# A spectral block on one core: its pipeline goes by one sequence instead of by two

## The chip, the cores and the metric

The kernel runs on one core of a Trainium2 chip. Its time is the device time of that core in microseconds (us), from the first to the last instruction of the program. Lower is better.

## The reference

Eight sequences of 3136 rows with 256 columns, all in float32:

```
X  = rfft(x, axis=1)                          # over the 3136 rows
Yr = Xr @ w_r - Xi @ w_i + b_r ;  Yi = Xr @ w_i + Xi @ w_r + b_i
Yr, Yi = soft_threshold(Yr, 0.01), soft_threshold(Yi, 0.01)
y  = irfft(Yr + i Yi, axis=1)
u  = y + real(fft(fft(y, axis=1), axis=2))    # over the rows and over the columns
un = (u - mean(u)) / sqrt(var(u) + 1e-6)      # along the columns
out = u + relu(un @ w_ch1) @ w_ch2            # w_ch1 256 x 1024, w_ch2 1024 x 256, float64
```

The transform of the rows of `y` is the thresholded spectrum itself, so the second transform over the rows needs no work of its own: the spectrum, transformed over the columns, is added to `y`.

## The kernel before

A transform of 3136 = 64 * 49 points goes in two stages, with n = 49 n1 + n2. The frequencies are held in 32 units; a unit has one k1 and its mirror, with 50 slots. Work passes through DRAM scratch between stages, because each stage wants another axis on the 128 partitions. The steps, each a generator in the program:

- `p1` (the first pair: `p1_first`): the sum over n1. The 128 partitions of a tile hold the 64 n1 of **two sequences**; a chunk is two values of n2 (128x512). One matmul against a table, the result (`ev`) is stored to `ad` (for the first eight units of the first pair to `a0`).
- `p2_f2`: the sum over n2, by units: `af` is loaded from `ad` (98 rows: n2 and real/imaginary), matmuls of 98x100 give the spectrum `X` and the sum of its parts `Xs`.
- `p2_w`: the complex product in three real ones (`g_w`), bias and soft threshold, giving `Y`.
- `p2_mix`: the transform of `Y` over the columns (`g_mix`, `mq`), stored to `md`.
- `p2_yt`, `p2_g2`: `Y` transposed (`g_yt`), the inverse sum over k2 (`g_g`, one matmul of 512 columns: a unit of two sequences), copied to `bev` and stored to `bd`.
- `p3_norm`: the inverse sum over n1: loads `bf` from `bd` and `mt` from `md`, a matmul, `ut` = the result + `mt`, then the norm. `p3_tr` transposes the normed `mt` (`g_ut`, giving `uth` and `utl`); `p3_mlp1` and `p3_mlp2` are the MLP in groups of up to four n2 (512 tokens): matmuls into `h`, ReLU to `hh` and `hl`, matmuls into `o`, the sum into `ut`, the store.

The frequencies go in eight steps of four units of two sequences. A step's product gives 128x400 tiles.

Precision: a float32 operand is split into a higher and a lower float32r part (`sc.copy` to the higher, a subtraction on VectorE by `lo_v` or GpSimd by `lo_g` to the lower), and `mm3` multiplies in three passes. Some work of the first pair, which runs while no MLP does, takes float32 as it is (first stage, `g_mix`, `g_g`), in one instruction pair without the splits. The MLP's float64 weights come as integer words; `split_double` makes them into two parts, in 16 blocks with eight VectorE instructions each.

What sets the order: each generator yields times of an emission clock (`T` = 10000 for a pair), and a heap merges them; so an engine's queue holds the steps of several pairs interleaved. While pair p is in its MLP (clock p + 2 to p + 3), pair p + 1 goes through `p2` and pair p + 2 through `p1`. Each engine runs its queue in order. All DMAs are issued by SyncE (SP), in order too; `behind(key)` queues a load behind a named earlier one. Buffers are few: `mt` 2, `bf` 2, `bh`/`bl` 2, `mq` 1, `X` 1, `ut` 6, and four PSUM tiles `g` for everything but the MLP.

The host permutes the rows back at the end. Nothing of that is in the time.

Of the kernel before, what the change touches and what calls it, by code (L numbers as in the profile page):

```python
# [10 lines left out]
F32 = mybir.dt.float32  # L11
# [7 lines left out]
N = 3136          # sequence length, 64 * 49; n = 49 * n1 + n2, k = k1 + 64 * k2  # L19
# [4 lines left out]
U = 32            # units of frequencies: unit u holds k1 = u and its mirror 64 - u (u = 0: k1 = 0 and 32)  # L24
# [8 lines left out]
# Constants by shape.  # L33
# [4 lines left out]
def slot_freqs(u):  # L38
    """(full index t of each slot, sign of the imaginary part against the canonical half)"""
    if u == 0:  # L40
        t = np.concatenate([64 * np.arange(25), 32 + 64 * np.arange(25)])
        return t, np.ones(50)
    t = np.concatenate([u + 64 * np.arange(25), N - (64 - u) - 64 * np.arange(24)])
    return t, np.concatenate([np.ones(25), -np.ones(24)])


def rows_n1():
    """n1 of the rows (half, n1) of the last stage: the second half runs backwards"""
    a = np.arange(32)
    return np.stack([a, 63 - a])  # L50


def tables():
    n1 = np.arange(N1)
    n2 = np.arange(N2)
    fwd = np.zeros((2, N1, 2, U, 2))      # s n1 | c u s
    inv = np.zeros((2, U, 2, 2, 2, 32))   # c u s | h s n1
    n1h = rows_n1()
    for s in range(2):
        for u in range(U):  # L60
            ph = 2 * np.pi * ((n1 * u) % N1) / N1
            if u == 0:
                alt = np.where(n1 % 2, -1.0, 1.0)
                fwd[s, :, 0, 0, s] = 1.0
                fwd[s, :, 1, 0, s] = alt
                inv[0, 0, s, :, s] = 1.0
                inv[1, 0, s, :, s] = np.where(n1h % 2, -1.0, 1.0)
            else:
                fwd[s, :, 0, u, s] = np.cos(ph)
                fwd[s, :, 1, u, s] = -np.sin(ph)  # L70
                phh = 2 * np.pi * ((n1h * u) % N1) / N1
                inv[0, u, s, :, s] = 2 * np.cos(phh)
                inv[1, u, s, :, s] = -2 * np.sin(phh)
# [27 lines left out]
    cs = np.stack([np.cos(ph), np.sin(ph)], 1)      # p | which, e  # L101
    cs[0, 1, 0] = 1.0       # the row of d = 128
# [3 lines left out]
    first = np.concatenate([fwd[:, :, :, :8].reshape(128, 32), fwd[:, :, :, 8:].reshape(128, 96)], 1)  # L106
# [9 lines left out]
# The emission's schedule, and which engine takes which part.  # L116
PAR = dict(f2w0=1.0, w00=1.069, ww0=0.988, f2w=0.395, w0=0.569, ww=0.36, end0=0.847, end=0.853, p1a=1.155, p1w=0.854, late=0.2, mlag=0.874, nrm=-1.239, tr=-0.993, yt=0.022, yts=0.185, g2=0.35, mx=0.372, mxs=0.394, cva=1.2, cvw=0.62, p1b=-0.428, p1bw=0.58, xl0=2, al0=0, y0=4, cve=1, bev=2, bf=2, mbuf=1, xsb=1, al1=0, y1=2, mxe=0, mmc=3, elg=0, f1fp=1, ev0=0, ev1=1, xe0=0, ye0=0, bev0=0, xs0=0, wc=1.291, cf=0.686, xm=3, xsm=0, mqb=1, bevb=2, evb=2, xfb=2, afb=4, eob=2, ksb=2, utb=6, tihb=1, ehb=1, hb=2, w0f=0, m0f=1, g0f=1, xm0=2, xsm0=0, xalt=1, fa=3, fs=0.6, p1c=-0.09, p1cw=0.87, trx=0, mql=0, bk=3)
# [3 lines left out]
def spectral_block(ctx: ExitStack, tc: tile.TileContext, x, w_ri, b_ri, w1, w2,  # L121
# [3 lines left out]
    NP = NB // 2  # L125
# [5 lines left out]
    dr = ctx.enter_context(tc.tile_pool(name="dr", bufs=2, space=DRAM))  # L131
# [10 lines left out]
    def copy(which, i=0):  # L142
        """0: ScalarE, 1: in turns, 2: VectorE"""
        return va.tensor_copy if which == 2 or which == 1 and i % 2 else sc.copy

# [4 lines left out]

    Q = PAR
    T = 10000       # the clock of the emission: a pair's step
    UTB = Q["utb"]
    AFB = Q["afb"]
    MLAG = PAR["mlag"]
    st_eng = nc.sync

# [1 line left out]
    def split_double(name, h, l, sl, src):  # L159
        """Float64 words (as int32 pairs) in two float32r parts: the upper word's 20 bits of the  # L160
        significand with the exponent, in float32, and the next 24 bits of the lower word, scaled.
        What float32's range doesn't hold becomes zero or its largest."""
# [4 lines left out]
        behind(Q["bk"], out=raw, in_=src)  # L167
# [18 lines left out]
        cve = gp if PAR["cve"] else va  # L186
        cve.tensor_sub(d, wf, h[sl].bitcast(F32))
        cve.tensor_add(l[sl], d, rf)

    # The first pair's transforms take float32 as it is: the later pairs' run beside an MLP.  # L190
# [13 lines left out]
    def load_consts():  # L204
# [11 lines left out]
        if not Q["w0f"]:  # L216
            for name in ("wr", "ws", "wd"):
                split(name, KF[name])
# [3 lines left out]
        if not Q["f1fp"]:  # L222
            yield Q["p1a"] * T - 100
        split("fwd", fwd_f)
        if Q["m0f"]:
            yield Q["wc"] * T
        # e = 0..127, the higher and the lower part; the lower part's place of e = 0 holds e = 128
# [5 lines left out]
        yield Q["wc"] * T  # L233
        if Q["w0f"]:
            for name in ("wr", "ws", "wd"):
                split(name, KF[name])
# [6 lines left out]
    bias = cp.tile([128, 2, 2], F32, name="bias")    # p | c, half  # L243
# [16 lines left out]
    xv = x.rearrange("b (n1 n2) d -> (b n1) n2 d", n2=N2)  # L260
# [10 lines left out]
    done = set()    # (phase, pair) whose stores to DRAM are all emitted  # L271
    now = [0]       # the clock
# [5 lines left out]
    chunks = [(i, min(2, N2 - i)) for i in range(0, N2, 2)]  # L278

    def n2_rows(t, n0, n):  # L280
        """Rows (c, unit, sequence) of n values of n2"""
        return t[n0:n0 + n].rearrange("n c u s d -> (c u s) n d")

    def p1_first():
        """First stage of the forward transform, over n1, for the first pair, in the later phases' room.
        It goes to memory in two parts: that of the first units ahead of the rest."""
        a0 = dr.tile([N2, 2, 8, 2, D], F32, tag="a0", bufs=1, name="a0")
        ad = dr.tile([N2, 2, U - 8, 2, D], F32, tag="ad0", bufs=1, name="ad0")
        a_dram[0] = lambda u: (a0, u) if u < 8 else (ad, u - 8)
# [8 lines left out]
        for tag, bufs, z in stores:  # L298
            outs += [(tag, bufs, z, i) for i in range(z)]
# [512 lines left out]
```

## Time and profile before

| what | value |
|---|---|
| median of 3 runs | 1960.67 us (1960.62 to 1965.03) |
| profiled execution: span | 1965.8 us, 33430 instructions; its own time is this span, there being one core |
| TensorE matmul / weight load busy | 1876.3 us (95%) / 1684.1 us (86%) |
| VectorE, ScalarE, GpSimd busy | 1282.5 us, 828.8 us, 664.7 us |
| DMA | 222.87 MB, 36.9% of 16 engines' time |
| mean granted TensorE clock | 0.975 |

The profile's page cuts the span in 40 slices of 49 us and gives each engine's busy share in tenths, with the clock granted to TensorE. Matmuls overlap in the records, so a pace is read from the distance between the starts of neighbours and not from the length of one. "L148" is line 148 of the kernel. Behind an instruction stands how long its engine sat idle before it and who ended that.

### The profile page before, as it was taken

The page shows a single profiled execution, that of the slowest core. Times are in us where ns is not written, and L with a number is a line of the kernel's source. Part 1 is how long each engine was busy: PE and PEld are TensorE (multiplying, and loading weights), DVE is VectorE, ACT ScalarE, POOL GpSimd, SP SyncE. Part 2 cuts the span into 40 slices and gives each one's busy share as a digit, 9 for nine tenths or more (in the row PEclk, how much of TensorE's full clock was granted, in tenths as well). Part 3 has the DMA queues.
Part 4 walks back from the last instruction along what each step waited for, and adds up shares of the span by engine and source line. Part 5 has one row for each costly group of instructions (what it writes and reads, how often), then busy time and mean ns, then how long its engine had stood idle before and what let it go on. Part 6 is the DMA issues. An engine that isn't in the chain of part 4 may idle for free. (4 is left out here: it accounts for less than half of the span.)

```text
span 1965.8 us, 33430 instructions
## 1 busy us (share of the span) xinstructions
PE 1876.3 (95%) x11706; PEld 1684.1 (86%) x11706; DVE 1282.5 (65%) x2819; ACT 828.8 (42%) x1867; POOL 664.7 (34%) x1070
## 2 busy tenths in 40 slices
PE   6878859999999999999999999999999999999999
PEld 4666628999888989999999999999989999999999
DVE  1778535577777865677777765677777765555543
ACT  4445434345445444444444434444444433322222
POOL 0446233335434444433333323233333322111110
PEclk8888979999999999999999999999999999999999
DMA  9655465334444455333333232233333132222110
GB/s 282 196 166 157 142 200 161 109 103 141 126 132 139 135 167 152 103 104 98 105 92 103 84 115 82 72 98 94 109 94 92 60 118 83 65 65 65 57 41 25
DMA packets 153231, 222.87 MB, mean 113 GB/s; under 512 B 17504, under 2 KB 91112, under 8 KB 152936
## 3 DMA queue, kind: packets, MB, share of 16 engines
q1 hardware_dynamic: 153064, 220.74, 36.9%
q8 instruction: 93, 1.52, 0.3%
q14 instruction: 74, 0.61, 0.1%
HBM read 117.91 MB, written 102.76 MB: 112 GB/s over the span
## 5 line engine op out<-in xcount | busy, mean ns | idle before, releaser
L732 DVE SCALAR_TENSOR_TENSOR hl<-h,hh 128x512 fp32r<-128x512 f32 (+1 forms) x416 | 272.1, 655 | 271.6 <-ACT hh L731 271.0
L731 ACT ACTIVATE hh<-h 128x512 fp32r<-128x512 f32 (+1 forms) x416 | 238.0, 572 | 484.9 <-PE h L149 418.2
L148 PE MATMUL o<-w2h,hl 128*128 128x256 f32 x1568 | 435.7, 287 | 4.8 <-DVE hl L732 4.6
L149 PE MATMUL o<-w2h,hh 128*128 128x256 f32 x1568 | 430.2, 283 | 0.0
L147 PE MATMUL o<-w2l,hh 128*128 128x256 f32 x1568 | 396.7, 287 | 1.3 <-ACT hh L731 1.3
L147 PE MATMUL h<-utl,w1h 128*128 128x512 f32 (+1 forms) x832 | 322.3, 387 | 0.0
L148 PE MATMUL h<-uth,w1l 128*128 128x512 f32 (+1 forms) x832 | 317.1, 381 | 0.0
L149 PE MATMUL h<-uth,w1h 128*128 128x512 f32 (+1 forms) x832 | 316.9, 381 | 0.0
L148 PEld LDWEIGHTS o<-w2h,hl 128*128 128x128 f32 x1568 | 298.1, 190 | 12.0 <-DVE hl L732 6.8
L149 PEld LDWEIGHTS o<-w2h,hh 128*128 128x128 f32 x1568 | 298.3, 190 | 4.4
L147 PEld LDWEIGHTS o<-w2l,hh 128*128 128x128 f32 x1568 | 288.1, 190 | 16.1 <-ACT hh L731 1.6
L140 POOL TENSOR_TENSOR bl<-bf,bh 128x512 fp32r<-128x512 f32 x104 | 129.5, 1246 | 425.7 <-ACT bh L672 418.1
L409 PEld LDWEIGHTS g_f<-tff,af 98*128 98x128 f32 x1024 | 146.4, 203 | 40.1 <-issue 20.5
L409 PE MATMUL g_f<-tff,af 98*128 98x100 f32 x1024 | 152.8, 283 | 26.1 <-issue 10.9
L149 PEld LDWEIGHTS h<-uth,w1h 128*128 128x128 f32 x832 | 156.7, 188 | 23.5
L147 PEld LDWEIGHTS h<-utl,w1h 128*128 128x128 f32 x832 | 157.7, 190 | 16.6
L148 PEld LDWEIGHTS h<-uth,w1l 128*128 128x128 f32 x832 | 157.8, 190 | 14.4
L140 POOL TENSOR_TENSOR Xl<-xx,Xh 128x400 fp32r<-128x400 f32 (+1 forms) x96 | 100.6, 1051 | 110.3 <-ACT Xh L421 95.4
L694 DVE TENSOR_SCALAR mt<-ut,ag,rs 128x256 f32<-128x256 f32 x196 | 86.1, 478 | 48.6 <-POOL rs L692 48.0
L483 POOL TENSOR_TENSOR Y<-y,m 128x400 f32<-128x400 f32 x48 | 56.3, 1172 | 177.8 <-DVE m L482 172.9
L480 DVE SCALAR_TENSOR_TENSOR y<-g_w,bias,ks 128x400 f32<-128x400 f32 x128 | 80.4, 628 | 51.7 <-PE g_w L149 51.5
L140 POOL TENSOR_TENSOR xl<-xf,xh 128x512 fp32r<-128x512 f32 (+1 forms) x50 | 63.7, 1273 | 117.6 <-ACT xh L347 117.5
(154 smaller groups left out, 3615.1 us busy)
## 6 DMA issues: line engine op xcount, KB each, us to landing
bd<-bev SPq DMA_DIRECT2D x128, 196.0 KB
bf<-bd SPq DMA_DIRECT2D x92, 256.0 KB
out_dram<-ut SPq DMA_DIRECT2D x92, 256.0 KB
af<-ad SPq DMA_DIRECT2D x120, 196.0 KB
xf<-in_x SPq DMA_DIRECT2D x80, 256.0 KB
ad<-ev SPq DMA_DIRECT2D x72, 256.0 KB
mt<-md SPq DMA_DIRECT2D x208, 64.0 KB
mt<-md SPq DMA_DIRECT2D x92, 128.0 KB
```

The lines of the kernel that those rows point to most:

```text
L140: gp.tensor_sub(out_, full, hi.bitcast(F32))
L147: te.matmul(o, lh, rl, start=start, stop=False)
L148: te.matmul(o, ll, rh, start=False, stop=False)
L149: return te.matmul(o, lh, rh, start=False, stop=stop)
L409: te.matmul(g[:, b:b + 100], af[:, s * D + k * 128:s * D + k * 128 + 128], tff[:, ui], start=True, stop=True)
L480: va.scalar_tensor_tensor(y1, gw, bias[:, c, o:o + 1], ks, op0=ALU.add, op1=ALU.add)
L483: (va if 2 * o + c < (Q["y1"] if p else Q["y0"]) else gp).tensor_sub(y[:, o, :, c, :], y1, m)
L694: va.tensor_scalar(mt[:, j], ut[:, j], ag[:, j, 0:1], rs[:, j], op0=ALU.subtract, op1=ALU.mult)
L731: sc.activation(hh[:, :w], h[:, :w], AF.Relu)
L732: va.scalar_tensor_tensor(hl[:, :w], h[:, :w], 0.0, hh[:, :w].bitcast(F32), op0=ALU.max, op1=ALU.subtract)
```

## The change

- **A tile's rows hold two values of n2 of one sequence.** In `p1` the two halves of the 128 partitions are n2 = m and n2 = 25 + m of the same sequence (m = 0..23); the odd one left, n2 = 24, is done for two sequences together. A sequence has 12 chunks instead of 25 for a pair, and every second sequence one more of half the width.
- **A step of frequencies is eight units of one sequence**; there are four steps for a sequence. Where the second index of a tile was the sequence it is now the unit's half.
- **The stages overlap by sequence**: eight of them go through the pipeline instead of four pairs, with a clock of their own (`STEP0`, `STEP1`, `STEP`, `START1`, `LEAD`). While sequence b is in its MLP, b + 1 ends its `p2` and b + 2 begins it.
- **Loads and stores that took a whole tile now take its halves**: `xf`, `ev`, `bf` in two DMAs each, `mt` of one part (two n2) in six instead of three. `af` comes in one load of four units (392 KB) instead of one a unit (196 KB); `tff` and `tif` are loaded for every sequence. All DMAs together: 1203 before, 1813 after, counted in SyncE's queue.
- **`p2_g2`**: the two halves of a tile are different units with different tables, so its matmuls have 256 columns instead of 512, and there are twice as many (672 instead of 288 in `mm3`).
- **Without splits** is now the work of the first sequence alone (first stage also of the second) instead of the first pair's.
- The loads that prefetch are queued behind other loads than before; `split_double`'s 16 blocks stand at clock 1.2 to 1.7 of a sequence's clock instead of 1.2 to 1.82 of a pair's.
- The scratch for dynamic DMA is 1 KB, and `af` has three buffers of 4 KB instead of four of 2 KB; `ad`, `bd`, `md` have four buffers in DRAM instead of two.

The core of the diff:

```diff
-T = 10000       # a pair's step
+T = 10000
+SHAPE0, STEP0 = (1.0, 1.069, 0.988), 0.13
+SHAPE, STEP1, STEP = (0.395, 0.569, 0.36), 0.2, 0.25
+START1, LEAD = 1.77, 1.48
...
-    def clock2(p, q):
-        f2w, w0, ww = SHAPE if p else SHAPE0
-        late = Q["late"] * T if p == 1 else 0
-        step = (T * (END if p else END0) - late) / (8.6 + w0 + ww)
-        return p * T + T + late + step * q, step, f2w, w0, ww, w0 + ww
+    def clock2(b, q):
+        f2w, w0, ww = SHAPE if b else SHAPE0
+        step = T * ((STEP0, STEP1)[b] if b < 2 else STEP)
+        t0 = T * (1.0, START1)[b] if b < 2 else T * (b + 2 - LEAD)
+        return t0 + step * q, step, f2w, w0, ww, w0 + ww
...
-                if G32[p]:
-                    te.matmul(g[:98], tih[:, ui], yh, start=True, stop=True)
-                else:
-                    mm3(g[:98], tih[:, ui], til[:, ui], yh, yl)
+                for v in range(2):
+                    cols = slice(v * D, v * D + D)
+                    t = 2 * (i % 2) + v
+                    if b == 0:
+                        te.matmul(g[:98, cols], tih[:, t], yh[:, cols], start=True, stop=True)
+                    else:
+                        mm3(g[:98, cols], tih[:, t], til[:, t], yh[:, cols], yl[:, cols])
...
-                nc.sync.dma_start(out=bf[:, :w].rearrange("p (n d) -> p n d", d=D),
-                                  in_=bd[n0:n0 + n].rearrange("n c u s d -> (c u s) n d"))
-                nc.sync.dma_start(out=mt[0:64, :n], in_=mpn[:, n0:n0 + n, :])
-                for j in range(n):
-                    nc.sync.dma_start(out=mt[64:128, j], in_=mmn[:, 48 - n0 - j, :])
+                for r, (bb, n2) in enumerate(src):
+                    nc.sync.dma_start(out=bf[r * 64:r * 64 + 64, :w].rearrange("p (n d) -> p n d", d=D),
+                                      in_=n2_rows(b_dram[bb], n2, n))
+                for r, (bb, n2) in enumerate(src):
+                    nc.sync.dma_start(out=mt[32 * r:32 * r + 32, :n], in_=mpn[:, n2:n2 + n, :])
+                    for j in range(n):
+                        nc.sync.dma_start(out=mt[64 + 32 * r:96 + 32 * r, j], in_=mmn[:, 48 - n2 - j, :])
...
-    nc = _bacc.Bacc("TRN2", target_bir_lowering=False, num_devices=1)
+    nc = _bacc.Bacc("TRN2", target_bir_lowering=False, num_devices=1, dynamic_dma_scratch_size=1024)
```

Where the change moves instructions, at three places. First TensorE just ahead of the MLP's first matmul (into `h`), before: `g_ut` and `g_g` are the first pair's own, `g_f` the second and third pair's first stage.

```order
L712 MATMUL g_ut<-ident,mt 128x128 x2
L343 MATMUL g_f_2723<-xf,fwd_f 128x256
L712 MATMUL g_ut<-ident,mt 128x128 x2
L147 MATMUL g_f_2730<-xl,fwdh 128x512
L148 MATMUL g_f_2730<-xh,fwdl 128x512
L149 MATMUL g_f_2730<-xh,fwdh 128x512
L147 MATMUL g_g_2751<-bl,invh 128x512
L148 MATMUL g_g_2751<-bh,invl 128x512
L149 MATMUL g_g_2751<-bh,invh 128x512
L147 MATMUL h<-utl,w1h 128x512
```

The same place after; `g_w`, `g_yt` and `g_f` are here the second sequence's `p2`.

```order
L150 MATMUL g_w<-Xl,wdh 128x400
L151 MATMUL g_w<-Xh,wdl 128x400
L152 MATMUL g_w<-Xh,wdh 128x400
L150 MATMUL g_g_1934<-bl,invh 128x512
L151 MATMUL g_g_1934<-bh,invl 128x512
L152 MATMUL g_g_1934<-bh,invh 128x512
L604 MATMUL g_yt<-ident,Y 100x128
L416 MATMUL g_f_1984<-tff,af 128x100 x4
L150 MATMUL h<-utl,w1h 128x512
```

A quarter of the second sequence's product (36 matmuls into `g_w`) has moved in between the first sequence's last `g_mix` and the first `h`; before, nothing of the second pair's `p2` stood there.

Second, SyncE's queue where a later pair's last rows of `md` are stored and its `mt` loads begin, before:

```order
L571 DMA md_85<-mq 25x2x1024
L572 DMA md_85<-mq 24x2x1024
L270 DMA xf<-in_x 128x512
L667 DMA mt<-md_82 64x256
L669 DMA mt<-md_82 64x256
L352 DMA ad_90<-ev 128x2x256
L664 DMA bf<-bd_86 128x2x256
L270 DMA xf<-in_x 128x512
L752 DMA out_dram<-ut 128x512
L752 DMA out_dram<-ut 128x256
L667 DMA mt<-md_85 64x512
```

And after:

```order
L573 DMA md_89<-mq 25x2x1024
L574 DMA md_89<-mq 24x2x1024
L664 DMA bf<-bd_90 64x2x256 x3
L668 DMA mt<-md_89 32x512
L670 DMA mt<-md_89 32x256 x2
L668 DMA mt<-md_89 32x512
L670 DMA mt<-md_89 32x256 x2
L754 DMA out_dram<-ut 128x512
```

Between the last store of `md` and the first load from it stood eight DMAs; now there are three, and the loads of a part are six.

Third, VectorE while the first frequencies are worked on. Before, the blocks of `split_double` (`cv_w`, from `raw_w`) begin behind the first step's fourth and last product (`y`):

```order
L483 TENSOR_TENSOR Y<-y_434,m 128x8x50
L480 SCALAR_TENSOR_TENSOR y_467<-g_w,bias,ks 128x400
L170 TENSOR_SCALAR cv_w_mt<-raw_w_604 128x256
L175 TENSOR_SCALAR cv_w_ut<-raw_w_604 128x256
L181 TENSOR_SCALAR cv_w_mt<-raw_w_604 128x256
L516 SCALAR_TENSOR_TENSOR ef<-Y,mask 128x8x25 x2
```

After, they begin behind the first step's `xs` and `Xl`, and two whole blocks and most of a third stand there ahead of the first `y`:

```order
L443 TENSOR_TENSOR xs<-g_f_275,im 128x200
L144 TENSOR_TENSOR Xl<-g_f_275,Xh 128x2x200
L169 TENSOR_SCALAR cv_w_mt<-raw_w_375 128x256
L174 TENSOR_SCALAR cv_w_ut<-raw_w_375 128x256
L180 TENSOR_SCALAR cv_w_mt<-raw_w_375 128x256
L171 TENSOR_SCALAR cv_w_mt<-cv_w_mt 128x256
L172 TENSOR_SCALAR cv_w_mt<-cv_w_mt 128x256
L175 TENSOR_TENSOR cv_w_ut<-cv_w_ut,cv_w_mt 128x256
```

The splitting has moved ahead of the first product's bias and threshold on this engine.

More of the change, by code (lines that the diff above doesn't have):

```diff
@@ L105, in tables @@
     mask[:, 1] *= -1.0
[L106 removed]
+    first = np.concatenate([fwd[..., :8].reshape(128, 32), fwd[..., 8:].reshape(128, 96)], 1)
     out = dict(
@@ L215, in load_consts @@
             va.scalar_tensor_tensor(KF[name], wi, sign, KF["wr"], op0=ALU.mult, op1=ALU.subtract)
-        if not Q["w0f"]:
-            for name in ("wr", "ws", "wd"):
-                split(name, KF[name])
+        for name in ("wr", "ws", "wd"):
+            split(name, KF[name])
         yield 0.99 * T
@@ L326, in p1_first, with p1 @@
+        done.add(("a0", 0))
+        yield from after(("af", 1))
+        for o, i in rest:
+            with tc.issue_after(af_ld[1]):
+                st_eng.dma_start(out=o, in_=i)
         done.add(("a", 0))
-    def p1(p):
-        if p == 0:
+    def p1(b):
+        if b == 0:
             yield from p1_first()
             return
-        ad = dr.tile([N2, 2, U, 2, D], F32, tag="ad", name=f"ad{p}")
-        a_dram[p] = lambda u: (ad, u)
-        a, b = {1: (Q["p1a"] - 1, Q["p1w"]), 2: (Q["p1c"], Q["p1cw"])}.get(p, (Q["p1b"], Q["p1bw"]))
-        for ci, (n0, n) in enumerate(chunks):
-            yield T * (p + a + b * ci / len(chunks))
+        for i in (b, b + 1)[:1 + (b % 2 == 0)]:
+            if i not in a_dram:
+                ad = dr.tile([N2, 2, U, D], F32, tag="ad", bufs=4, name=f"ad{i}")
+                a_dram[i] = lambda u, ad=ad: (ad, u)
+        todo = chunks + [(NM - 1, 1)] * (b % 2 == 0)
+        t0, width = (1.4, 0.38) if b == 1 else (b - 0.3, 0.75)
+        for ci, (m, n) in enumerate(todo):
+            yield T * (t0 + width * ci / len(todo))
@@ L443, in p2_f2, with p2_w @@
                 put(sc.copy, [Xsh], xs)
-                put(lo_v if ui < (Q["xsm"] if p else Q["xsm0"]) else lo_g, [Xsl, Xsh], xs)
-    def p2_w(p):
-        for q in range(8):
-            base, STEP, F2W, W0, WW, M0 = clock2(p, q)
+                put(lo_g, [Xsl, Xsh], xs)
+    def p2_w(b):
+        for q in range(4):
+            base, STEP, F2W, W0, WW, M0 = clock2(b, q)
             base += STEP * W0
@@ new lines, in p2_mix, with rows, rows2 @@
+    def p2_mix(b):
+        md = dr.tile([2 * (NH + 64), D], F32, tag="md", bufs=4, name=f"md{b}")
+        mpd, mmd = m_dram[b] = md[0:NH + 64], md[NH + 64:]
+        both = md[0:2 * (NH + 63)].rearrange("(a r) d -> a r d", a=2)
+        def rows(d, first, nj, n):
+            return d[first:first + 64 * nj].rearrange("(j k) d -> j k d", k=64)[:, 0:n]
+        def rows2(first, nj):
+            return both[:, first:first + 64 * nj].rearrange("a (j k) d -> j a (k d)", k=64)[:, :, 0:4 * D]
+        for q in range(4):
+            base, STEP, F2W, W0, WW, M0 = clock2(b, q)
+            u0 = 8 * q
@@ new lines, in spectral_block, with clock3, p3_norm @@
+    groups = [[(4 * i, 4) for i in range(6)], [(4 * i, 4) for i in range(4)] + [(16 + 3 * i, 3) for i in range(3)]]
+    parts_of = {z: [(i, min(2, z - i)) for i in range(0, z, 2)] for z in (3, 4)}
+    normed, uts, uthl, hhl = {}, {}, {}, {}
+    def clock3(b, g0):
+        nt = NM - 1 + b % 2
+        return (b + 2 + g0 / nt) * T, T * 4 / nt
+    def p3_norm(b):
+        for gi, (g0, z) in enumerate(groups[b % 2]):
+            t0, T3 = clock3(b, g0)
+            for i, n in parts_of[z]:
+                yield t0 + T3 * (NRM + i / 4)
+                yield from after(("b", b), ("m", b))
+                m = g0 + i
```

464 lines of the change are left out of this document (216 added, 248 removed).

## Prediction

> **What bounds the kernel now.** I read the page's head and its slices first, then the busy times of stages, then the order of instructions in time at the seams between stages.
>
> ```profile
> span 1965.8 us, 33430 instructions
> PE 1876.3 (95%) x11706; PEld 1684.1 (86%) x11706; DVE 1282.5 (65%) x2819; ACT 828.8 (42%) x1867; POOL 664.7 (34%) x1070
> PE   6878859999999999999999999999999999999999
> DVE  1778535577777865677777765677777765555543
> PEclk8888979999999999999999999999999999999999
> DMA  9655465334444455333333232233333132222110
> ```
>
> TensorE is the bound from the seventh slice on, and only there. In the first six it is neither fully busy nor at full clock, while DMA and then VectorE are high. The seams give the stages:
>
> ```profile
> 4.16 5.66 PE L310 MATMUL g_f<-xf,fwd 128*128 128x512 f32 x8 [4.16 <-DMA xf<-in_x]
> 9.98 17.84 PE L310 MATMUL g_f<-xf,fwd 128*128 128x512 f32 x42 [0.16 <-DMA xf<-in_x]
> 47.57 0.68 PE L147 MATMUL g_w<-Xsl,wrh 128*128 128x400 f32 x1
> 264.72 1.18 PE L536 MATMUL g_mix<-csf,ef 128*100 128x129 f32 x4 [4.36 <-DVE mq L549]
> 288.64 0.69 PE L712 MATMUL g_ut<-ident,mt 128*128 128x128 f32 x2 [7.30 <-DMA xf<-in_x]
> 300.31 0.63 PE L147 MATMUL h<-utl,w1h 128*128 128x512 f32 x1
> ```
>
> The first product begins at 47.6, the first pair's last `g_mix` ends near 265.7, the MLP begins at 300.3. Busy time by these stages (TensorE, weight loads, VectorE, ScalarE, GpSimd, then clock, DMA share, GB/s; the second row is a part of the first):
>
> ```profile
> 47.60:265.70 218.10, 176.97 (x865) 137.62 (x865) 149.64 (x369) 106.98 (x292) 93.18 (x114) 0.89 0.56 168
> 75.00:175.00 100.00, 80.41 (x395) 62.33 (x393) 83.83 (x219) 51.33 (x143) 55.65 (x67) 0.88 0.56 171
> 265.70:300.30 34.60, 18.14 (x39) 9.80 (x39) 10.26 (x26) 11.11 (x21) 13.17 (x19) 0.65 0.70 216
> 300.30:1700.00 1399.70, 1387.03 (x9004) 1276.44 (x9003) 989.03 (x2130) 613.60 (x1364) 515.02 (x815) 1.00 0.36 108
> 1700.00:1966.00 266.00, 261.85 (x1715) 241.57 (x1713) 126.74 (x279) 74.80 (x147) 38.69 (x112) 1.00 0.17 53
> ```
>
> From 300.3 on TensorE stands idle for 12.7 us of 1400 and 4.2 of 266, at a clock of 1.00: what stands behind the first `h` costs its own pace. Ahead of it, 300 us are spent on a chain of engines that wait for each other. So the change is worth what it does to the head, less the work that it moves out of it, plus what it costs in the filled stage.
>
> **The head.** It has three parts, and each is sized by its own row.
>
> *To the first product*: 25 chunks run from 4.2 to 27.8, held by `x` (two sequences, 6.4 MB); now 13 chunks and half the bytes, 23.6 * 13/25 = 12.3 us, so 11.3 less. I leave the rest (stores, `af`, `f2`) alone: 47.6 - 11.3 = 36.3.
>
> *The steps*: a step's `g_mix` ends 1.95 step widths after its product begins (places 1.069 and 3.02 of a step), so eight steps took 7 + 1.95 widths in 218.1 us, or 24.4 us a width. Four steps take 4.95 widths, 120.6 us. VectorE must be able to do that. The 16 blocks of the weights' split are not halved. They are eight groups of 16 instructions, the longest and the shortest of them:
>
> ```profile
> L183 DVE SCALAR_TENSOR_TENSOR cv_w_ut<-cv_w_mt,cv_w_ut 128x256 f32<-128x256 int32 x16 | 8.7, 547 | 0.2
> L179 DVE TENSOR_SCALAR cv_w_ut<-cv_w_ut 128x256 int32<-128x256 int32 x16 | 5.1, 316 | 0.1
> ```
>
> The eight sum to 55.2 us. Of the stage's 149.6 the rest, 94.4, is halved: 47.2 + 55.2 = 102.4 us in 120.6, a share of 0.85. In the row from 75 to 175, where the splits ran, VectorE did 83.8 in 100. So the step's width can just stay as it is; at the whole stage's share (0.686) it would be 149 us, which is the other bound.
>
> *To the first `h`*: 34.6 us of latency, kept (the stores of `md`, the loads, the norm, the transposition). The second sequence's products that now stand there (36 * 0.195 = 7 us, priced below) fill idle time. The first `h` comes at 36.3 + 120.6 + 34.6 = 191.5, which is 108.8 earlier. Bounds: with VectorE at 0.686 it is 36.3 + 149 + 34.6 = 220; with all halved, 150.
>
> **The work moved behind the first `h`.** Its prices are start-to-start distances at full clock:
>
> ```profile
> 247.70 0.36 PE L147 MATMUL g_w<-Xl,wdh 128*128 128x400 f32 x1
> 247.89 0.36 PE L148 MATMUL g_w<-Xh,wdl 128*128 128x400 f32 x1
> 302.35 0.40 PE L147 MATMUL h<-utl,w1h 128*128 128x512 f32 x1
> 302.58 0.39 PE L148 MATMUL h<-uth,w1l 128*128 128x512 f32 x1
> 304.14 0.28 PE L149 MATMUL o<-w2h,hh 128*128 128x256 f32 x1
> 304.26 0.28 PE L147 MATMUL o<-w2l,hh 128*128 128x256 f32 x1
> 1206.42 0.42 PE g_f L409 x4
> 1262.39 0.44 PE g_yt L608 x4
> ```
>
> 512 columns take 0.232 us (over several neighbours), 400 take 0.195, 256 take 0.12; the chain's two rows give 0.105 for a record of `f2` (two records make a matmul, 0.21) and 0.11 for a transposition. Counted in the two orders behind the first `h` (before, after): `f2` 384, 428 (+44 * 0.21 = 9.2); products 864, 972 (+108 * 0.195 = 21.1); `g_yt` 384, 447 (+63 * 0.11 = 6.9); `g_mix` 192, 224 pairs of 256 and some 129 columns (+32 * 0.18 = 5.8); first stage in three passes 141, 210 (+69 * 0.232 = 16.0); `g_g` 288 of 512 columns against 672 of 256 (80.6 - 66.8 = +13.8, of which 2.7 is that two halves cost 0.24 and a whole 0.232). The MLP, `g_ut` and the inverse over n1 are the same. Sum: +72.8 us. This leaves 72.8 - 108.8 = **-36.0**.
>
> **The filled stage.** VectorE's load per us of TensorE's work hardly changes, since the instructions are the same ones; the same holds for ScalarE and GpSimd, at lower shares. What changes is the distance at each sequence's seam, from the last `g_mix` to its own first transposition:
>
> ```profile
> 719.12 0.28 PE L539 MATMUL g_mix<-cs,eh 128*100 128x256 f32 x1
> 755.20 0.38 PE L712 MATMUL g_ut<-ident,mt 128*128 128x128 f32 x2
> 727.80 1.86 SPq L572 DMA_DIRECT2D md<-mq  x1
> 284.75 0.69 DVE L677 TENSOR_TENSOR ut<-g_g,mt 128x512 f32<-128x512 f32 x1 [11.18 <-DMA mt<-md]
> 1170.70 2.25 DMA mt<-md
> ```
>
> Before, the second pair had 36 us there, all of it covered by other matmuls. Counted in the new order at the prices above, TensorE has 22 to 27 us of work between the two for sequences 1 to 7. What the path needs was to be seen bare once, for the first pair: from 265.7 to 288.64, 23 us, with the last wait of 11.18 on `mt`, at a DMA share of 0.70. At the second pair's seam the last store of `md` went out 8.7 us behind the `g_mix`; with 2.25 us to land (the chain's row for a load of `mt`, taken for the store too), six loads (3 us to issue, 2.25 to land) and 3.9 us from `ut` to the transposition (284.75 to 288.64) that is 20. So need and cover are about equal. I take 1.5 us for each of seven seams, **+10** (ends: 0 where 20 is right; +70 where the need is 10 us above the cover). An engine that runs in order gives such a wait on: VectorE stuck at `ut` delays `hl`, and TensorE's matmuls into `o` stand behind that.
>
> **SyncE's queue.** It takes 610 more DMAs. The times of an issue (least, median, longest, in ns), and its longest wait in total, for a buffer that TensorE frees:
>
> ```profile
> L669 SPq DMA_DIRECT2D mt<-md x196: 444/588/1572, 281.7 to 1904.3; - x196
> L667 SPq DMA_DIRECT2D mt<-md x104: 444/450/1996, 281.1 to 1903.8; - x104
> SPq L667 <- PE g_ut L712: 156.4, 58, 5.1
> ```
>
> At 0.45 to 0.59 us, 1813 issues are 820 to 1070 us of some 1940; so SyncE has the time, and I put the extra at nothing but the 1.5 us a seam for three more loads, which is in the +10. What covers it is that loads go out a part ahead; where that is gone, each part of 104 pays up to 4 issues, 2 us. The Trainium skill's page "DMA: Bandwidth & Descriptors", section "Rules for kernel authors", speaks against the change: two transfers to disjoint partition halves serialise, one of 128 partitions should be used, and below 64 KB one pays mostly overhead (`mt` now goes in pieces of 32 and 64 KB). By it the 20 us path would grow by the split loads' time, which no row here shows; the rival below has the bound.
>
> **Costed at nothing:** the DMA scratch. All packets but 167 go through one queue:
>
> ```profile
> q1 hardware_dynamic: 153064, 220.74, 36.9%
> ```
>
> Should that queue draw on the scratch, the issues would get longer than the rows above, which is rival 3. The larger `af` loads and the doubled table loads (64 more of 153 KB, 10 MB of 223) lie in a stage whose DMA share is 0.36. The end is the same MLP alone, idle 4 us.
>
> **The sum.** 1965.8 - 36.0 + 10 = 1939.8 for a profiled execution. That one lay 5.1 us above the median of the runs shown; against the median it is 1934.7, and I say 1936.
>
> **The rivals.**
> 1. *VectorE holds the head's steps.* For it: the share of 0.85 that I need was held for 100 us but not longer, and two blocks of the split now stand ahead of the first threshold, waiting for their own loads. Against: VectorE's longest idle time in the stage was ten waits behind `mq`, a single buffer, and they come half as often (us in total, times, longest):
>
> ```profile
> DVE mq L549 <- ACT mq L543: 36.9, 10, 9.6
> ```
>
>    At a share of 0.686 the first `h` is at 220 and the time 1936 + 28 = 1964: no change.
> 2. *The seams stall* (the other side). The path needs more than its cover, through the stores of `md` behind GpSimd and three queued `bf` loads that wait for buffers. At 32 us, 8 to 10 a seam, seven seams cost 56 to 70 instead of 10: 1982 to 1996, slower. It turns the sign from 36/7, about 5 us a seam. For it: 36 us of cover became 24. Against: the bare 23 us were measured at twice the DMA load.
> 3. *SyncE becomes the bound.* If half of the parts pay their four more issues, 52 * 2 = 104 us: 2040. Against: its queue waits for buffers to come free, which means that it is ahead. The rule of the Trainium skill named above speaks for it.
> 4. *More than half*: with the early DMA load halved, the first product comes earlier and the steps shrink; the first `h` at 165 gives 1910.
>
> **How the numbers follow.** A measurement of this kernel tells 0.3% (6 us) from no change. Forecast, from 1912 to 1954: 0.62. Rival 1, 1955 to 1966: 0.15. Rival 2: 0.15, of which a third ends below 1975. Rival 3: 0.04. Rival 4, at or below 1911: 0.04. Faster 0.66, same 0.15, slower 0.19. The range 1908 to 1976 leaves out the far part of rivals 2 and 3 and a little of 4.
>
> **What would show it.** First `h` between 183 and 205 us, four steps in some 120 us with VectorE above 0.8 busy: the head is right. TensorE idle behind the first `h` at 25 us or so in all, in short waits at seven seams on `ut`, `mt` or `hl`: the seams are right; waits of 5 us and more there are rival 2. A first `h` beyond 210 is rival 1; waits on loads away from the seams, with SyncE issuing without pause, rival 3. I would be wrong as a whole if the clock stayed low after the head, or if `f2` of later sequences waited for `ad`, whose stores now come closer ahead of their loads.

## The result: slower by half a per cent

The kernel after takes 1975.66 us (median of 6 runs, 1973.73 to 1980.2), the kernel before 1964.56 us in the 6 runs beside it (1960.62 to 1968.95). The ratio is 1.0055, with a 95% interval of 1.004 to 1.0071: some 11 us slower, where 1936 was forecast. The profiled execution spans 1974.1 us against 1965.8.

The page of the kernel after, its head and the slices that were shown of before:

```profile
span 1974.1 us, 35182 instructions
PE 1861.2 (94%) x12115; PEld 1709.3 (87%) x12115; DVE 1330.2 (67%) x2903; ACT 850.3 (43%) x1888; POOL 710.1 (36%) x1103
PE   4875799989999999999999999999999999999999
DVE  3973777767766776766667776766677766675543
PEclk7896899999999999999999999999999999999999
DMA  8466544344343543435443454435433333223210
```

The head is shorter, as it should be: TensorE is full from the sixth slice on (but for one slice of 8), not from the seventh. But where half of 300 us would be three slices, it lost one and a half. The seams, from the timeline of TensorE (start, duration, instruction, idle time ahead of it and its releaser):

```profile
4.61 5.08 PE L310 MATMUL g_f<-xf,fwd 128*128 128x512 f32 x8 [4.61 <-DMA xf<-in_x]
12.60 2.81 PE L310 MATMUL g_f<-xf,fwd 128*128 128x512 f32 x6 [2.92 <-DMA xf<-in_x]
16.34 4.96 PE L310 MATMUL g_f<-xf,fwd 128*128 128x512 f32 x12 [0.93 <-DMA xf<-in_x]
30.96 7.12 PE L416 MATMUL g_f<-tff,af 98*128 98x100 f32 x32 [9.65 <-DMA tff<-c_tf]
50.29 1.15 PE L416 MATMUL g_f<-tff,af 98*128 98x100 f32 x4 [12.21 <-DMA af<-ad]
51.14 0.68 PE L150 MATMUL g_w<-Xsl,wrh 128*128 128x400 f32 x1
181.24 1.07 PE L535 MATMUL g_mix<-csf,ef 128*100 128x129 f32 x4
208.25 0.66 PE L713 MATMUL g_ut<-ident,mt 128*128 128x128 f32 x2 [11.80 <-DMA xf<-in_x]
223.34 0.47 PE L150 MATMUL h<-utl,w1h 128*128 128x512 f32 x1
```

The first product begins at 51.1 (forecast 36.3), the last `g_mix` of the first sequence ends at 182.3, the MLP begins at 223.3 (forecast 191.5). Now the span cut at the first `h`, in the kernel before and then in the kernel after (length; TensorE, weight loads, VectorE, ScalarE, GpSimd busy; clock, DMA share, GB/s):

```profile
0.00:300.31 300.31, 227.47 (x990) 166.09 (x991) 166.69 (x411) 140.38 (x357) 110.96 (x143) 0.85 0.64 192
300.31:1965.80 1665.49, 1648.86 (x10717) 1518.01 (x10715) 1115.78 (x2408) 688.40 (x1510) 553.72 (x927) 1.00 0.33 99
```

```profile
0.00:223.34 223.34, 140.02 (x623) 109.28 (x624) 130.70 (x307) 85.87 (x211) 84.32 (x112) 0.79 0.64 175
223.34:1974.10 1750.76, 1721.21 (x11495) 1600.04 (x11493) 1199.50 (x2597) 764.40 (x1677) 625.74 (x992) 0.99 0.39 111
```

Length less busy time is TensorE's idle time. Ahead of the first `h` it was 72.8 us and is 83.3; behind it 16.6 and now 29.6. So 87 us of TensorE's busy time left the head, and none of the head's waiting did. That waiting rose by 10.5 us, the waiting behind the first `h` by 13.0, and the busy time fell by 15.1 (1876.3 to 1861.2): together the 8.3 us of the two spans. The busy time fell because the work costs TensorE less behind the first `h`: 72.4 us were added there for the 87.4 that left. One difference is the form: a product of 512 columns in float32 as it is took 0.85 us in the first chunks before (42 records in 17.84 us, two to a product), and in three passes at 0.232 it takes 0.70. How much of the 15.1 us that makes up was not traced.

### The profile page after: what moved, and what is told of

Its sections match the earlier page's. It is cut to its first block, busy times and chain, and to the rows that moved or that the text cites. A ratio compares the mean times of both kernels' runs of the same rounds, so it can differ in the third digit from the quotient of the medians.

```text
span 1974.1 us, 35182 instructions
## 1 busy us (share of the span) xinstructions
PE 1861.2 (94%) x12115; PEld 1709.3 (87%) x12115; DVE 1330.2 (67%) x2903; ACT 850.3 (43%) x1888; POOL 710.1 (36%) x1103
## 4 chain that ended last, share of the span: by engine, by line
PE 80%; DMA 7%; DVE 7%; SPq 2%; issue 1%; ACT 1%; POOL 0%; DVEq 0%; ACTq 0%; POOLq 0%
PE o L151 9%; PE o L150 9%; PE o L152 8%; PE h L150 8%; PE h L152 8%; PE h L151 8%; PE g_f L416 4%; PE g_w L150 3%; PE g_w L151 3%; PE g_w L152 3%; PE g_g L150 2%; PE g_g L152 2%; PE g_g L151 2%; PE g_yt L604 2%; PE g_ut L713 2%; DMA md<-mq 2%
## 5 line engine op out<-in xcount | busy, mean ns | idle before, releaser
L151 PEld LDWEIGHTS o<-w2h,hl 128*128 128x128 f32 x1568 | 296.3, 189 | 16.6 <-DVE hl L733 12.1
L416 PE MATMUL g_f<-tff,af 98*128 98x100 f32 x1024 | 152.6, 280 | 32.3 <-DMA af<-ad 16.6
L147 POOL TENSOR_TENSOR xl<-xf,xh 128x512 fp32r<-128x512 f32 (+1 forms) x75 | 97.4, 1298 | 221.6 <-ACT xh L359 213.4
L678 DVE TENSOR_TENSOR ut<-g_g,mt 128x512 f32<-128x512 f32 x104 | 68.3, 657 | 106.8 <-PE g_g L152 68.1
L147 POOL TENSOR_TENSOR Xsl<-xs,Xsh 128x200 fp32r<-128x200 f32 x120 | 77.4, 645 | 155.3 <-ACT Xsh L425 132.6
L147 POOL TENSOR_TENSOR Xl<-xx,Xh 128x400 fp32r<-128x400 f32 (+1 forms) x96 | 106.8, 1115 | 71.5 <-ACT Xh L425 67.8
L695 DVE TENSOR_SCALAR mt<-ut,ag,rs 128x256 f32<-128x256 f32 x196 | 90.8, 502 | 46.2 <-POOL rs L693 45.9
```

The costliest lines, as they stand in the source:

```text
L147: gp.tensor_sub(out_, full, hi.bitcast(F32))
L151: te.matmul(o, ll, rh, start=False, stop=False)
L416: te.matmul(g[:, o:o + 100], afs[s][:, ui * D + k * 128:ui * D + k * 128 + 128], tfs[s][:, ui], start=True, stop=True)
L678: va.tensor_add(ut[:, :n], g[:, :w].rearrange("p (n d) -> p n d", d=D), mt[:, :n])
L695: va.tensor_scalar(mt[:, j], ut[:, j], ag[:, j, 0:1], rs[:, j], op0=ALU.subtract, op1=ALU.mult)
```

## The experiments

My theory after the result: the forecast behind the first `h` holds, and the head misses in three places with a cause each, namely a first scratch tile `a0` that covers one step instead of two, VectorE's splitting of the weights, and the third sequence's first stage in the gap ahead of `h`. The rivals: the split loads, the seams, and the single buffer of `mq`. All runs, from their profiles (us), with the ratio of the times to the kernel before:

| kernel | first product | steps | gap to `h` | first `h` | behind it | ratio (95%) |
|---|---|---|---|---|---|---|
| before | 47.6 | 218.3 | 34.4 | 300.3 | 1665.5 | 1 |
| after | 51.1 | 131.2 | 41.0 | 223.3 | 1750.8 | 1.0055 (1.004 to 1.0071) |
| e1: after, `a0` of two steps | 44.7 | 132.1 | 41.2 | 218.0 | 1752.4 | 1.0043 (1.0029 to 1.0057) |
| e2: after, product earlier | 41.5 | 144.9 | 40.5 | 226.9 | 1752.2 | 1.0101 (1.0072 to 1.013) |
| e3: after, split cut short | 49.9 | 121.7 | 40.5 | 212.1 | 1749.6 | 1.0017 (1.0 to 1.0034) |
| e3b: before, split cut short | 48.2 | 217.6 | 35.3 | 301.1 | 1663.2 | 1.0004 (0.9986 to 1.0022) |
| e4: before, loads split | 47.2 | 217.0 | 35.9 | 300.1 | 1666.1 | 1.0025 (1.0011 to 1.0038) |
| e5: after, third sequence later | 50.6 | 130.4 | 37.3 | 218.4 | 1753.4 | 1.0074 (1.0052 to 1.0096) |
| e6: after, `mq` twice | 50.8 | 131.6 | 42.1 | 224.5 | 1749.3 | 1.0075 (1.0054 to 1.0095) |
| e6b: before, `mq` twice | 47.8 | 192.9 | 39.0 | 279.6 | 1664.0 | 0.9883 (0.9861 to 0.9904) |
| e7: after, e1 + e5 + e6 | 45.1 | 131.0 | 39.7 | 215.9 | 1758.0 | 1.0058 (1.0038 to 1.0078) |
| e8: after, e3 + e6 | 50.3 | 118.5 | 42.2 | 210.9 | 1752.7 | 0.9997 (0.9985 to 1.001) |
| e9: before, scratch of 1 KB | 47.8 | 217.2 | 35.4 | 300.3 | 1660.9 | 1.0002 (0.9985 to 1.0018) |
| e10: after, second sequence later | 51.7 | 123.7 | 51.6 | 226.9 | 1756.8 | 1.0098 (1.0075 to 1.0121) |

"Steps" runs from the first product to the end of the first sequence's (before: pair's) last `g_mix`. The stages are read from one execution each. In before, e3b, e9 and e6b, whose work behind the first `h` is the same, that stage varies from 1660.9 to 1665.5 us; so a difference of less than 5 us in that column tells little by itself.

### Undoing or doing one part: e4 and e9

e4 gives the kernel before the split loads of the kernel after, 404 more DMAs (the expectation says 416): `bf` in two of 64 rows, and `mt` in pieces of 32 rows, of which one kind is shown:

```diff
-  nc.sync.dma_start(out=mt[0:64, :n], in_=mpn[:, n0:n0 + n, :])
+  for r in range(2):
+      rs_ = slice(32 * r, 32 * r + 32)
+      nc.sync.dma_start(out=mt[32 * r:32 * r + 32, :n], in_=mpn[rs_, n0:n0 + n, :])
```

> The kernel before with one part of the change alone: bf loaded in two DMAs of 64 rows and mt in six of 32 rows instead of one and three (416 more DMAs). My sum put this at nothing but 1.5 us of issue at a seam: the time stays within 0.3% of the kernel before (at most 6 us more), and the 1665 us behind the first h stay within 5 us. The rule of the Trainium skill (DMA: Bandwidth & Descriptors, Rules for kernel authors: no halves in two transfers) and rival 3: 416 issues at 0.45 us come on top wherever SyncE has no slack, and some tens of us are lost in waits for bf and mt.

Measured: behind the first `h` 0.6 us more, the time up by 0.25% (0.11 to 0.38), 2 to 7 us. SyncE's issues of `mt` (two sizes) and of `bf` in this kernel, then of `bf` in the kernel before (least, median, longest, ns):

```profile
L673 SPq DMA_DIRECT2D mt<-md x392: 302/419/1567, 278.0 to 1905.7; - x196
L671 SPq DMA_DIRECT2D mt<-md x208: 302/412/1648, 277.4 to 1905.2; - x104
L666 SPq DMA_DIRECT2D bf<-bd x208: 465/596/2093, 269.1 to 1877.5; - x104
```

```profile
L664 SPq DMA_DIRECT2D bf<-bd x104: 326/387/2432, 270.0 to 1875.6; - x104
```

Halves of `mt` take 0.42 and 0.41 us to issue where the whole ones took 0.59 and 0.45, so the queue pays less than twice. A half of `bf` takes 0.60 us where the whole took 0.39, so there it pays three times. Rival 3, tens of us in waits for these loads, did not come. The rule of the Trainium skill that I weighed ("DMA: Bandwidth & Descriptors", "Rules for kernel authors": transfers to disjoint halves of the partitions serialise) is not what decides here: whatever two halves cost between them, other work covers all but those few us. Whether the halves serialise no run here shows.

e9 is the kernel before with `dynamic_dma_scratch_size=1024` and nothing else.

> The kernel before with the DMA scratch of 1 KB and nothing else. Theory A, the size of the scratch costs and gives no time: the steps in 217 to 219 us, the first h at 300, the time within 0.3% of 1964.6; then the gain of e6b belongs to the second buffer of mq alone. Theory B, the scratch itself brings part of that gain or costs something: a time more than 0.3% away.

Measured: 1.0002 (0.9985 to 1.0018), every stage within 1.1 us but the last, which is 4.6 us shorter in the profile and not in the time. The scratch costs and gives no time here, as theory A has it.

### The first product: e1 and e2

e1 lets `a0` hold 16 units, two steps of the kernel after. The other units are then stored behind the loads of both steps.

```diff
-  a0 = dr.tile([N2, 2, 8, D], ...)
+  a0 = dr.tile([N2, 2, 16, D], ...)
...
-  yield from after(("a0" if b == 0 and q == 0 else "a", b))
+  yield from after(("a0" if b == 0 and q < 2 else "a", b))
```

> The changed kernel, with the first sequence's rows of 16 units (two steps) instead of 8 in the part of the scratch that is stored first (a0). Theory A, order and data: the first product (51.1 us in the changed kernel) is held by the second step's f2, which stands ahead of it on TensorE and waits 12.2 us for rows that are stored late. Then it comes at 39 to 42, the first h at 210 to 214 instead of 223.3, and the time falls by 9 to 13 us. Theory B, VectorE: the split of the weights sets the pace of the steps, so they take longer by what the product gains, and the first h stays at 220 or later. Theory C, the single buffer mq and its stores set the pace of the steps: the steps keep their 131 us, so as A.

Measured: the first product comes 6.4 us earlier, the first `h` 5.3, and the profile is 3.7 us shorter; the intervals of the two ratios overlap. That is theory A's direction at about half its size: it had the first product at 39 to 42 and 9 to 13 us of the time. TensorE's start in e1:

```profile
31.33 7.97 PE L416 MATMUL g_f<-tff,af 98*128 98x100 f32 x36 [10.03 <-DMA af<-a]
44.73 0.70 PE L150 MATMUL g_w<-Xsl,wrh 128*128 128x400 f32 x1 [2.56 <-POOL Xsl L147]
```

The wait of 12.21 for `af` from `ad` is gone. It had stood ahead of the first product, because the order puts the second step's first matmuls there. The 10 us ahead of the first `f2` stay (9.65 in the kernel after, 10.03 here).

e2 puts the product ahead of those matmuls by the table of the order alone. All that follows the product in a step moves forward with it.

```diff
-SHAPE0, STEP0 = (1.0, 1.069, 0.988), 0.13
+SHAPE0, STEP0 = (1.0, 0.99, 0.988), 0.13
```

> The changed kernel, with the first sequence's product emitted at 0.99 of a step instead of 1.069, which puts the first product ahead of the second step's f2 on TensorE and changes nothing else on purpose. Theory A: the first product comes at 39 to 41 us; the second step's f2 still waits for its rows until about 50, so that only a part, 3 to 10 us, arrives at the first h (213 to 220). Theory B: the threshold behind the product waits on VectorE behind the blocks of the split, and the first h stays at 221 to 224.

Measured: the first product at 41.5, 9.7 us earlier, and the steps 13.7 longer. The first `h` comes at 226.9, later than either theory has it. The waits come back inside the steps (TensorE's waits there: in total, times, longest):

```profile
PE g_w L150 <- DVE y L478: 7.6, 3, 3.1
PE g_f L416 <- DMA af<-ad: 7.0, 1, 7.0
PE g_w L150 <- POOL Xl L147: 6.8, 1, 6.8
```

### The steps: e3, e3b, e6, e6b, e8

e3 leaves seven of eight VectorE instructions of each block of `split_double` out, so that the MLP's weights are other numbers; e3b does so in the kernel before.

```diff
-  va.tensor_scalar(t, hi, 0x7FFFFFFF, None, op0=ALU.bitwise_and)
...
-  gp.tensor_add(l[sl], d, rf)
+  gp.tensor_add(l[sl], d, wf)
```

> The changed kernel, leaving out seven of the eight VectorE instructions of each of the 16 blocks of the weights' split (48 of 55 us of VectorE); the loads, ScalarE's and GpSimd's part stay, and the MLP's weights are other numbers. Theory B: VectorE, 94 of 131 us busy in the steps, set their length: the steps take 90 to 105 us, the first h comes at 180 to 197, the time falls by 27 to 43 us. Theories A and C: the first product stays at 49 to 51 and the steps at 120 to 131; the first h stays at 210 or later, the time falls by at most 13 us.

> The kernel before, with the same part of the split left out. Its VectorE is 0.69 busy in the steps. Theory B says that there was room for the split there: the first h comes 0 to 12 us earlier than 300.3, and the time falls by less than 12 us, less than half of what the same does to the changed kernel. Theory C says the same small gain for both.

Measured: the four steps fall from 131.2 to 121.7, the eight steps of before from 218.3 to 217.6. The steps of the kernel after in full and in their two parts, then those of e3 (columns as above):

```profile
51.14:182.31 131.17, 97.80 (x466) 77.51 (x465) 93.87 (x230) 56.93 (x149) 55.91 (x69) 0.85 0.58 162
51.00:100.00 49.00, 40.16 (x221) 36.01 (x219) 45.82 (x113) 23.12 (x66) 28.71 (x39) 0.89 0.44 126
100.00:182.00 82.00, 57.47 (x244) 41.34 (x245) 48.05 (x118) 33.74 (x83) 27.20 (x31) 0.83 0.66 184
```

```profile
49.87:171.60 121.73, 94.48 (x466) 77.31 (x466) 61.23 (x132) 54.43 (x149) 51.47 (x69) 0.84 0.62 176
```

Until 100 us VectorE does 45.8 in 49: it is the bound there, with the blocks of the split. Behind that it does 48 in 82. e3 bears this out: from the first product to VectorE's first `ef`, in the first step, 22.4 us became 15.9, so 6.4 of the 9.5 us were lost there. The split's 33 us of busy time on VectorE cost 9.5 us of the steps here, and 0.7 in the kernel before, which is within the scatter of that stage (217.0 to 218.3 over before, e3b, e4 and e9). Theory B is right about where, but not about how much: it had the steps at 90 to 105 and 27 us of the time or more, and the time fell by 10 (1975.66 to 1965.56).

e6 and e6b give `mq` two buffers. For the room, e6b takes the scratch of 1 KB too; by e9 the scratch alone gives nothing.

```diff
-  mq = sb.tile([100, 2, 4, 2, 128], F32, tag="mq", bufs=1, name="mq")
+  mq = sb.tile([100, 2, 4, 2, 128], F32, tag="mq", bufs=2, name="mq")   # e6b: by its table of parameters
```

> The changed kernel with two buffers for mq instead of one (8 KB more on a partition, which the smaller DMA scratch leaves room for). Theory C: ScalarE's and VectorE's first writes of mq wait for the stores of the step before (VectorE 23 us in 8 waits in the head), and this sets the steps' width of 26.5 us. Then the steps fall from 131 to 105 to 120 us, the first h comes 11 to 26 us earlier, the time falls by as much. Theory B, or a chain that is long by itself: the waits move to another instruction and the steps stay above 126 us.

> The kernel before with two buffers for mq, which fit only with the DMA scratch of 1 KB, so that this is also the scratch alone plus a buffer. Theory C: the steps fall from 218 us by 20 to 45, the time by as much. If the scratch costs anything at each DMA, the 1665 us behind the first h get longer; I expect them within 3 us.

Measured: nothing in the kernel after, and 25.4 us of the steps in the kernel before, which then runs at 0.9883 of its time. VectorE's longest waits in the steps, before, e6b, after and e6:

```profile
DVE mq L549 <- ACT mq L543: 35.8, 9, 9.6
```

```profile
DVE mq L549 <- ACT mq L543: 16.4, 9, 3.4
```

```profile
DVE mq L548 <- ACT mq L542: 15.3, 7, 5.8
DVE cv_w_mt L169 <- DMA raw_w<-in_w: 8.5, 3, 4.7
```

```profile
DVE mq L548 <- ACT mq L542: 13.7, 5, 8.5
DVE cv_w_mt L169 <- DMA raw_w<-in_w: 12.5, 3, 5.9
```

In the kernel before the second buffer takes 19.4 us out of that wait. In the kernel after it takes 1.6, and the wait for `raw_w` grows by 4.0. So this row does not by itself tell a lack of buffers: with two of them 16.4 and 13.7 us of it are left, as much as the kernel after had with one.

e8 has both edits, to see whether the split hides the second buffer's gain.

> The kernel after without seven of the eight VectorE instructions of each block of the weights' split (as in e3: the low parts are then left as they come), and with two buffers of mq. Theory A, VectorE's split hid what the second buffer gives, as both edits act on the same engine: the four steps in 105 to 110 us instead of 121.7 (e3), the first h near 198, the time 1952 or less. Theory B, the four steps are held by loads and by the length of the chain through the engines, not by VectorE: 118 to 123 us as in e3, the time 1962 to 1966.

Measured: 118.5 for the steps, 3.2 less than e3, with a gap 1.7 longer, and the time at 0.9997. Theory B: the second buffer gives next to nothing in the kernel after, with the split or without.

### The gap and the neighbours' first stages: e5, e7, e10

e5 starts the third sequence's first stage later, out of the gap; e10 moves the second's too.

```diff
-  t0, width = (1.4, 0.38) if b == 1 else (b - 0.3, 0.75)
+  t0, width = (1.4, 0.38) if b == 1 else (1.95, 0.5) if b == 2 else (b - 0.3, 0.75)   # e5
+  t0, width = (1.6, 0.25) if b == 1 else (2.0, 0.5) if b == 2 else (b - 0.3, 0.75)    # e10
```

> The changed kernel with the third sequence's first stage at clock 1.95 to 2.45 instead of 1.7 to 2.45, so that it stands behind the first sequence's steps instead of among them. Theory D, traffic: the 41 us from the last g_mix to the first h (34 us before) and a part of the steps are long because this stage's loads and stores share SyncE and the DMA engines with them. Then the last part falls to 33 to 37 us and the steps by up to 5, and the time by 5 to 12 us. Theory C (mq) and the plain latency of the chain: the first h moves by less than 3 us, and the time stays.

> The kernel after with the second sequence's first stage moved later, from place 1.40 to 1.60, so that most of it stands behind the last step of the first sequence and in the gap before the first h (and the third's first stage as in e5, behind that). Theory A, the four steps are held by TensorE's waits for that stage's loads and low parts (5.3 us for xl, 4.8 for xf and 2.3 for mq within the steps): steps 115 to 120 us instead of 131.2, latency 41 to 44, the first h at 208 to 212 and the time 1962 to 1968. Theory B, these waits cover for the chain of the step itself: steps 128 to 131, and the loads that now stand in the gap make the latency 45 or more; the time 1975 to 1985.

The steps and the gap in e10:

```profile
51.67:175.35 123.68, 95.45 (x449) 76.84 (x449) 90.46 (x228) 53.38 (x145) 55.81 (x66) 0.82 0.49 137
175.35:226.95 51.60, 25.90 (x92) 20.38 (x91) 16.75 (x38) 13.78 (x31) 16.78 (x26) 0.60 0.66 171
```

Measured: e5 shortens the gap by 3.7 us, as theory D has it, and the steps by 0.8; its time is no better. e10 takes 7.5 off the steps and puts 10.6 on the gap. The steps come out between the two theories, the gap and the time are B's, and the sum is slower: the second sequence's first stage does hold the steps up, but it stands worse at the one later place that was tried.

e7 joins e1, e5 and e6.

> The kernel after with three edits of its head together: the first scratch tile holds 16 units (as in e1), the third sequence's first stage starts later (as in e5), and mq has two buffers (as in e6). Theory A, the head's parts add up (first product -6.4, latency -4, mq 0): the first h at 213 to 215 instead of 223.3, the work behind it 1749 to 1753, the time 1966 to 1969. Theory B, the parts share one slack, so that a gain in one comes back as a wait in the next: the first h at 218 or later and the time 1972 or more, as with the first of them alone (1972.5).

Measured: the first `h` at 215.9, 7.5 earlier than in the kernel after, and 7.3 more behind it, so the time is the same (1975.71 us). Theory A has the head, to within 1 us of its range of 213 to 215, and theory B the time: TensorE's busy time behind the first `h` is 1727.7 instead of 1721.2. Part of that is work that the gap had held at no cost: 12 more matmuls of the third sequence's first stage stand behind the first `h`, 2.8 us at 0.232. The rest of the 7.3 us was not traced.

## Why the prediction was wrong

The step that failed is the head's sum, 36.3 + 120.6 + 34.6: all three terms were too small.

**The first product: 36.3 forecast, 51.1 measured (+14.8).** Two errors. The chunks were to end at 16.5 and ended at 21.3 (+4.8). I had called them held by `x`, but the row of before has 0.16 us of waiting in 42 records: TensorE was busy throughout. That part did scale, to 12.9 us of TensorE's time against 12.3. What came on top are two waits for `xf`, of 2.92 and 0.93 us, and a start 0.5 us later. In the chain that ended last the load behind the second of them goes out at 9.63, behind two stores of the first `ev` in SyncE's queue, and lands 6.6 us later; no run tested another order. And I "left the rest alone", 19.8 us from the last chunk to the first product. It became 29.8. TensorE's wait ahead of the first `f2` grew from 7.3 to 9.7, and the wait of 12.21 for the second step's `af` is new in its length, since `a0` keeps its eight units, which are one step now where they were two; e1 gives 6.4 of these 10 us back.

**The steps: 120.6 forecast, 131.2 measured (+10.6).** The width could "just stay as it is" if VectorE kept a share of 0.85. It reached 0.72 over the whole: 0.94 in the first 49 us and 0.59 behind. I had named the blocks of the split that moved ahead of the first threshold, and priced them as if their load could be spread evenly. e3 shows that term: without the split the width is as forecast (121.7). This is rival 1 at a third of its size.

My load for VectorE was wrong as well, to the other side. The 55.2 us of the split are a sum of lengths, and neighbours overlap in the records: e3b takes 47.5 us of these lengths out, and VectorE's busy time in the steps falls by 29.8 (149.6 to 119.8). So the forecast had 102.4 us of VectorE's time, and 93.9 were measured. The steps were too long all the same: the place of the split decided, and not the sum.

One doubt from the end of the prediction came true here, too. The second sequence's `f2` waits for `ad` shortly ahead of the first sequence's last `g_mix`, as TensorE's timeline and the chain that ended last show:

```profile
178.59 1.15 PE L416 MATMUL g_f<-tff,af 98*128 98x100 f32 x4 [4.39 <-DMA af<-ad]
```

```profile
170.78 2.54 DMA ad<-ev
173.35 5.11 DMA af<-ad
```

It is 4.4 us here and 3.3 in e3. In e10, whose steps are 7.5 us shorter, this wait stands in the gap instead, at 201.6, and takes 8.8 us. No run takes it out alone.

**The gap: 34.6 forecast, 41.0 measured (+6.4).** The path to `ut` is as it was: it takes 18.1 us, against 18.9 before. These are pieces of the chain that ended last, in the kernel after:

```profile
187.72 1.75 DVE mq L556
190.66 5.59 DMA md<-mq
198.48 1.84 DMA mt<-md
200.44 0.70 DVE ut L678
202.59 1.28 ACT L686
205.01 3.17 DMA xf<-in_x
```

The next piece is the transposition at 208.25. From `ut` to it are 7.8 us (before 3.9). The chain names a load of `xf` as what released it. But in e5, where that load does not stand there, a load of `bf` is named, and TensorE is idle for as long (11.55 us, here 11.80):

```profile
206.75 0.66 PE L713 MATMUL g_ut<-ident,mt 128*128 128x128 f32 x2 [11.55 <-DMA bf<-bd]
```

What grew is the norm between the two. Ahead of its first root ScalarE loads a table, in 1.28 us. Before, that was done ahead of `ut`; after, it stands behind an `Xsh` of the second sequence, and on the path. ScalarE in the kernel after, and then before (where `ut` begins at 284.75):

```profile
202.59 1.28 ACT L686 ACT_TABLE_LOAD   x1
203.89 0.29 ACT L686 ACTIVATE rs<-ag,eps_t 128x2 f32<-128x2 f32 x1
```

```profile
284.14 1.28 ACT L685 ACT_TABLE_LOAD   x1
```

That makes 1.5 of the 3.9 us. GpSimd does an `Xsl` of the second sequence between two instructions of the norm (1.2), and VectorE's two instructions that write `mt` took 1.68 us where they took 0.73 (1.0). No run tested these.

From the transposition to `h` are 15.1 us (before 11.7), behind products and a first stage that belong to the next two sequences. TensorE runs in order (in e2 the product, moved ahead of the `f2` that waits, began 9.7 us earlier), so what I called filling of idle time held the path up. e5 shows 3.7 of the 6.4 us as the third sequence's: it takes 3.4 off this last stretch and 1.1 off the one from `ut`, and loses 0.9 ahead of `ut`.

**The work moved out, +72.8, and the seams, +10: right.** 1748.3 us were forecast behind the first `h`; it took 1750.8. Of TensorE's work alone 72.4 us were added there (1648.9 to 1721.2), and its idle time rose by 13.0. All but one of the waits of 0.5 us and more lie in seven places, one for each later sequence, 28 to 62 us ahead of its first `h`; the longest is 4.5 us. They are the short ones that I described, on `hl` and `ut`:

```profile
PE o L151 <- DVE hl L733: 9.6, 11, 3.7
PE h L150 <- DVE hl L733: 6.4, 2, 4.5
PE o L150 <- ACT hh L732: 5.3, 4, 3.5
PE o L150 <- DVE ut L752: 2.8, 2, 1.4
```

Rival 2 (5 us and more at every seam) and rival 3 (SyncE) did not come; nor did rival 4. Of the doubts at the end, a clock that stays low did not come (it is 0.99 behind the first `h`), and `f2` waiting for `ad` came in the head but is not among the rows above. The DMA scratch at nothing was right (e9). The split loads "at nothing" was nearly so, with e4's 2 to 7 us in the kernel before.

**The sum.** 14.8 + 10.6 + 6.4 = 31.8 us of the head, and 2.5 behind it, are the 34.3 us from 1939.8 to 1974.1. The sign hung on the head alone: the work moved out and the seams cost 85.3 us behind the first `h`, so the head had to lose more than that, and it lost 77.0. My error was one of kind, three times over: I took the waiting in a stretch as given, or as shrinking with the work, and did not ask what the new order puts ahead of it in each engine's queue. Of the three terms, e1, e3 and e5 gave back 6.4, 9.5 and 3.7 us in their stages, each alone, 19.6 of the 31.8. They do not simply add up: e1 and e5 together (e7) bring the first `h` 7.5 us earlier and not 10.1, and e3 alone lowers the time clearly. Open, with places read from the timeline but tested by no run, are the other 8.4 us of the first product (the 4.8 of the chunks above all), 1.1 of the steps and 2.7 of the gap.

**A better kernel.** The gain on offer lay in the kernel before: e6b, with a second buffer of `mq`, begins its MLP 20.7 us earlier and moves no work at all (1664.0 us behind the first `h`). It takes 1938.86 us, 1.2% less than before and 1.9% less than after. The head and slices of its page:

```profile
span 1943.6 us, 33398 instructions
PE   6888859999999999999999999999999999999999
```

I had quoted that wait for `mq` as a reason why the steps of the changed kernel would be less held. In the kernel before, the row did name what to remove.

## What to carry to other kernels

When a pipeline's head is made half as long, cut its time into work and waiting first: work moved out of the head is paid again where the bounding engine is busy (here 72 us for 87), and the waiting on stores, loads and first results need not halve with the data. The gain is then the waiting that really goes, here none, and what the moved work saves, here 15 us, less the new waits. And where one row of waits names a single buffer as the longest wait in the head, try that buffer alone before changing the shape of the pipeline: it is one edit, and only the run tells whether the buffer was the cause.

## What was not expected of the hardware

- The granted clock did not set the length of the steps: it was 0.89 before and 0.92 in e9, and the steps took 218.3 and 217.2 us. In the gap it was lowest, 0.59 to 0.72 over the kernels after.
- An issue on SyncE did not go by the size of the DMA. Half the rows lowered the median for `mt` from 0.59 to 0.42 us and from 0.45 to 0.41, and raised it for `bf` from 0.39 to 0.60 (e4).
- VectorE's two instructions that write the first `mt` took 1.68 us in the kernel after, with a subtraction of GpSimd running beside them from 206.7 on, and 0.73 us before, with GpSimd idle. e5 has 1.66 us, again beside that subtraction.
